# Attention's feature sums on two half-array column tiles: an attention and mixture kernel on one Trainium2 core

## The chip, the cores and the metric

The kernel runs on one core of one Trainium2 chip. Its time is the device time of that core in microseconds (us). A core has a TensorE for matrix products (in the profile PE for the matmuls and PEld for the weight loads that precede them), a VectorE (DVE), a ScalarE (ACT), a GpSimd (POOL) and a SyncE (SP), from whose queue this kernel starts its transfers.

## What is computed

Attention with exponential features over 8 batches of 8 heads, 576 tokens and 64 values a head, then a gated feed-forward layer on the 4608 tokens. All is float32.

```python
def phi(x):
    proj = np.einsum('bhsd,df->bhsf', x, w_phi)          # 64 -> 128
    proj = proj - np.max(np.abs(proj), axis=-1, keepdims=True)
    return np.concatenate([np.exp(proj), np.exp(-proj)], axis=-1)
q_p, k_p = phi(q), phi(k)
kv  = np.einsum('bhsf,bhsd->bhfd', k_p, v)               # the sums of features and values
z   = np.sum(k_p, axis=2)
num = np.einsum('bhsf,bhfd->bhsd', q_p, kv)
den = np.einsum('bhsf,bhf->bhs', q_p, z)[..., None] + 1e-06
x = num / den                                            # as 4608 tokens of 512
xn = x / rms(x) * rms_g
out = (silu(xn @ w_gate) * (xn @ w_val)) @ w_out         # 512 -> 1536 -> 512
```

The change concerns `kv` and `z`. They are computed as one: the values carry a 65th column of ones, which gives `z`.

## The kernel before

Heads are taken two at a time, so attention has 32 pairs. A loop over the pairs keeps four of them in flight: in iteration i it runs `front` of pair i (transposes and projections of keys and queries), `mid` of pair i-1 (exponentials and the sums), `back` of pair i-2 (numerators and denominators) and `last` of pair i-3 (the division and the store). Each is a list of small functions with places between about 0 and 1 of an iteration; `_merge` runs them in the order of these places. `mid` is spread evenly from -0.2 to 1.1. Beside them go the decoding of weights and, from iteration 9 on, `fill` products of the feed-forward layer (lines L489 before). The framework then orders each engine's instructions once more, by what is ready, so the calls of one function needn't stay together in an engine's queue; the listings below are of this final order. After attention, which ends at about 485 us, come the feed-forward layer's first products (L565) and its last (L1259).

The 576 tokens of a head are 4 blocks of 128 (`T0`) and a rest of 64; the rests of the two heads share one block. For each sign sg of the exponent, `mid` adds up in the tile `acc` (128 features x 2 signs x 2 heads x 65): `kvr(sg)`, one product for the rests of both heads (`er` with `vr`, 130 columns), and `kv(h, sg)`, four products for a head's blocks (`ek` with `vm`, 65 columns). With `kvr` that is 2 + 16 = 18 products for a pair. In each, the exponentials (128 tokens x 128 features, float32) are the weight that is loaded into TensorE, and the values are streamed through. Their order in `mid` before is

```python
rexp, kexp(0), qexp("q", 0), kvr(0), kv(0, 0), kexp(1), qexp("r", 0),
qexp("q", 1), kv(1, 0), (kvr(1), kv(0, 1)), kv(1, 1), kvs_
```

`kexp` and `rexp` make the exponentials of the keys on ACT, `qexp` transposes the queries' projections on TensorE and makes their exponentials on ACT and their low parts on POOL. `kvs_` copies `acc` into the tiles kv0 or kv1 (high part on ACT, low part on DVE), which `back` reads. There is one `acc`; the buffers of `ek` are two, one for each head, so that the next pair's `kexp` needs the sums of this one done.

Of the kernel before, what the change touches and what calls it, by code (L numbers as in the profile page):

```python
# [58 lines left out]
def _split(nc, hi, lo, x, hi_copy=None, lo_eng=None):  # L59
    (hi_copy or nc.scalar.copy)(hi, x)  # L60
    (lo_eng or nc.vector).tensor_tensor(lo, x, hi.bitcast(F32), ALU.subtract)  # L61
# [21 lines left out]
def kernel(ctx: ExitStack, tc: tile.TileContext, q, k, v, w_phi,  # L83
                         w_gate, w_val, w_out, rms_g, out):
    nc = tc.nc
# [7 lines left out]
    T0 = S // 128  # L93
# [104 lines left out]
    make_identity(nc, ident)  # L198


    const.tile([128, 32], F32, name="pad0")
    wh = const.tile([128, 2 * F], F32R, name="wh")
    wl = const.tile([128, 2 * F], F32R, name="wl")
# [123 lines left out]
    def mid(pr):  # L327
        d = st[pr]
        y, vm, vr, (kh, kl) = d["y"], d["vm"], d["vr"], d["kv"]
        acc = ps_k.tile([128, 2, 2, D + 1], F32, name="acc")  # L330
        qh = big.tile([128, 2, 2, S], F32R, name="qh")
        ql = big.tile([128, 2, 2, S], F32R, name="ql")
        d.update(qh=qh, ql=ql)
        er = wk.tile([128, 2, F], F32, name="er")
        e = {}

        def kexp(h):
            e[h] = wk.tile([128, 2, T0, F], F32, name="ek")
            for sg in range(2):
                nc.scalar.activation(e[h][:, sg], y["k", h], AF.Exp, scale=1.0 - 2.0 * sg)  # L340

        def rexp():
            for sg in range(2):
                nc.scalar.activation(er[:, sg], y["r", 0][:, 0], AF.Exp, scale=1.0 - 2.0 * sg)


        def kvr(sg):
            nc.tensor.matmul(acc[:, sg].rearrange("p h d -> p (h d)"), er[:, sg],
                             vr.rearrange("p s d -> p (s d)"), start=True, stop=False)

        def kv(h, sg):
            for j in range(T0):
                nc.tensor.matmul(acc[:, sg, h], e[h][:, sg, j], vm[:, h, j],  # L353
                                 start=False, stop=(h == 1 and j == T0 - 1))

        def kvs_():
            av = acc.rearrange("p a h d -> p h a d")
            _split(nc, kh[:, :, :, 0:D + 1], kl[:, :, :, 0:D + 1], av)
            if pr == PR - 1:
                for x in (kh, kl):  # L360
                    nc.vector.tensor_copy(x[:, :, :, D + 1:128], x.bitcast(F32)[:, :, :, D:D + 1].broadcast_to([128, 2, 2, 127 - D]))


        def qexp(n, h):
            m = 4 if n == "q" else 1
            yp = ps_s.tile([128, 512], F32, name="sm")
            for j in range(m):
                src = y[n, h][:, j] if n == "q" else y[n, h][:, 1]
                nc.tensor.transpose(out=yp[:, j * 128:(j + 1) * 128], in_=src, identity=ident)  # L369
            if n == "q":  # L370
                hi, lo = qh[:, :, h, 0:SM], ql[:, :, h, 0:SM]
                eq = wk.tile([128, 2, 512], F32, name="eq")
                ei, yi = eq, yp
            else:
                hi, lo = qh[:, :, :, SM:S], ql[:, :, :, SM:S]
                eq = wk.tile([128, 2, 128], F32, name="eqr", bufs=1)
                ei = eq.rearrange("p a (h s) -> p a h s", h=2)
                yi = yp[:, 0:128].rearrange("p (h s) -> p h s", h=2)
            for sg in range(2):
                nc.scalar.activation(ei[:, sg], yi, AF.Exp, scale=1.0 - 2.0 * sg)  # L380
                nc.scalar.activation(hi[:, sg], yi, AF.Exp, scale=1.0 - 2.0 * sg)  # L381
                if n == "q":
                    for c in range(0, SM, SM // 2):
                        cs = slice(c, c + SM // 2)
                        nc.gpsimd.tensor_tensor(lo[:, sg, cs], ei[:, sg, cs], hi[:, sg, cs].bitcast(F32), ALU.subtract)  # L385
            if n != "q":
                nc.gpsimd.tensor_tensor(lo, ei, hi.bitcast(F32), ALU.subtract)  # L387

        return [
            rexp,  # L390
            lambda: kexp(0),
            lambda: qexp("q", 0),
            lambda: kvr(0),
            lambda: kv(0, 0),
            lambda: kexp(1),
            lambda: qexp("r", 0),
            lambda: qexp("q", 1),
            lambda: kv(1, 0),
            lambda: (kvr(1), kv(0, 1)),
            lambda: kv(1, 1),  # L400
            kvs_,
        ]

# [114 lines left out]
    for i in range(PR + 3):  # L518
        streams = []
        if i < PR:  # L520
            streams.append(_spread(front(i), -0.2, 0.7))
        if 0 <= i - 1 < PR:
            streams.append(_spread(mid(i - 1), -0.2, 1.1))
        if 0 <= i - 2 < PR:
            streams.append(back(i - 2))
        if 0 <= i - 3 < PR:
            streams.append(last(i - 3))
        dq += 0.8 if i < 10 else 1.1
        dl, decs = decs[:int(dq)], decs[int(dq):]
        dq -= int(dq)  # L530
        streams.append(dl)
        if i < PR:
            _merge(streams)
        if len(units) <= 6:
            landed(nc.vector if i < PR else nc.gpsimd)
        if i >= FIRST:
            quota += (N // TF * J1 * 2 - RES - TAIL) / (PR - FIRST) if i < PR else TAIL / 3
            nf = min(int(quota + 1e-6), len(units))
            quota -= nf
            now, units[:] = units[:nf], units[nf:]  # L540
            _merge([now] if i < PR else streams + [_spread(now, 0.0, 0.75)])
        load_x()
        if i + 2 < PR:
            load(i + 2)
        if i in (20, 22):
            raw_gv((i - 20) // 2)
# [113 lines left out]
    nc = Engines()  # L660
# [513 lines left out]
    nc = tc.nc  # L1174
# [155 lines left out]
```

## Time and profile before

| | |
|---|---|
| median of 2 runs | 1246.05 us (1245.63 to 1246.46) |
| the profiled execution | 1252.8 us, span 1251.0 us, mean granted clock of TensorE 0.992 |
| PE, PEld busy | 1219.3 us (97%), 1208.1 us (97%), 10355 records each |
| DVE, ACT, POOL busy | 1037.2 (83%), 803.9 (64%), 832.2 us (67%) |
| sums, `kv` (L353) | 1024 matmuls, busy 131.2 us, mean 269 ns of one |
| sums, `kvr` (L348) | 128 matmuls, busy 26.3 us, mean 287 ns of one |

In such a profile a line as `L353 PE MATMUL acc<-vm,ek 128x65` names the line of the kernel, the engine, the operation, the tile written and those read, and the shape streamed. Busy times of matmuls overlap: a matmul's record lasts from its start to the modelled end of its results, and the next starts long before. What one costs is therefore read from the distance between starts, not from its length. In rows of time order the first number is the start, the second the length of the whole merged group, and xN the count.

### The profile page before, as it was taken

The page shows a single profiled execution, that of the slowest core. Times are in us where ns is not written, and L with a number is a line of the kernel's source. Part 1 is how long each engine was busy: PE and PEld are TensorE (multiplying, and loading weights), DVE is VectorE, ACT ScalarE, POOL GpSimd, SP SyncE. Part 2 cuts the span into 40 slices and gives each one's busy share as a digit, 9 for nine tenths or more (in the row PEclk, how much of TensorE's full clock was granted, in tenths as well). Part 3 has the DMA queues.
Part 4 walks back from the last instruction along what each step waited for, and adds up shares of the span by engine and source line. Part 5 has one row for each costly group of instructions (what it writes and reads, how often), then busy time and mean ns, then how long its engine had stood idle before and what let it go on. Part 6 is the DMA issues. An engine that isn't in the chain of part 4 may idle for free. (4 is left out here: it accounts for less than half of the span.)

```text
span 1251.0 us, 28462 instructions
## 1 busy us (share of the span) xinstructions
PE 1219.3 (97%) x10355; PEld 1208.1 (97%) x10355; DVE 1037.2 (83%) x1498; ACT 803.9 (64%) x1867; POOL 832.2 (67%) x774
## 2 busy tenths in 40 slices
PE   8999999999999998999999999999999899999998
PEld 7988999989999998999999999999999899999998
DVE  6888977678788886687997887988775889999995
ACT  6887887768788786667666667756655443433432
POOL 3654654456556666674876766787655578888885
PEclk9998999999999998999999999999999899999999
DMA  5545565766665654686466656566544544444531
GB/s 151 130 132 147 136 202 147 192 171 165 178 172 141 181 150 152 219 255 198 133 196 189 205 187 214 177 196 191 180 138 130 182 149 155 153 135 141 167 116 51
DMA packets 199752, 206.55 MB, mean 165 GB/s; under 512 B 70334, under 2 KB 169790, under 8 KB 197436
## 3 DMA queue, kind: packets, MB, share of 16 engines
q1 hardware_dynamic: 199612, 204.73, 54.5%
q8 instruction: 82, 1.34, 0.4%
q14 instruction: 58, 0.48, 0.1%
HBM read 135.18 MB, written 69.49 MB: 164 GB/s over the span
## 5 line engine op out<-in xcount | busy, mean ns | idle before, releaser
L385 POOL TENSOR_TENSOR ql<-eq,qh 128x256 fp32r<-128x256 f32 x256 | 215.6, 873 | 94.7 <-issue 59.0
L565 PE MATMUL B<-xo,w 128*128 128x256 f32 x1458 | 195.5, 278 | 2.5 <-DVE c L565 1.8
L565 PEld LDWEIGHTS B<-xo,w 128*128 128x128 f32 x1458 | 180.0, 188 | 4.0 <-DVE c L565 2.6
L61 POOL TENSOR_TENSOR xo<-st,xo 128x768 fp32r<-128x768 f32 x52 | 122.3, 2366 | 35.4 <-ACT xo L60 31.7
L314 DVE TENSOR_REDUCE mx<-pp 128x4 f32<-128x512 f32 (+1 forms) x160 | 101.0, 633 | 52.7 <-PE pp L312 51.2
L60 ACT CAST xo<-st 128x768 fp32r<-128x768 f32 x54 | 43.5, 836 | 150.1 <-DVE st L1209 73.7
L565 PE MATMUL E<-xo,w 128*128 128x256 f32 x972 | 137.7, 277 | 0.0
L565 PE MATMUL A<-xo,w 128*128 128x256 f32 x972 | 137.7, 277 | 0.0
L353 PE MATMUL acc<-vm,ek 128*128 128x65 f32 x1024 | 131.2, 269 | 0.0
L353 PEld LDWEIGHTS acc<-vm,ek 128*128 128x128 f32 x1024 | 127.3, 193 | 0.0
L565 POOL TENSOR_TENSOR h<-h,c 128x256 f32<-128x256 f32 x81 | 65.7, 811 | 91.3 <-ACT h L565 68.9
L565 PEld LDWEIGHTS A<-xo,w 128*128 128x128 f32 x972 | 123.5, 188 | 0.3
L565 PEld LDWEIGHTS E<-xo,w 128*128 128x128 f32 x972 | 123.4, 188 | 0.1
L381 ACT ACTIVATE qh<-sm 128x512 fp32r<-128x512 f32 (+1 forms) x192 | 96.9, 505 | 0.0
L61 POOL TENSOR_TENSOR xo<-w,xo 128x768 fp32r<-128x768 f32 x36 | 90.9, 2524 | 7.4 <-ACT xo L60 7.4
L310 PE MATMUL pp<-wh,th 128*128 128x256 f32 x288 | 87.7, 306 | 3.4 <-DVE yk L317 1.2
L380 ACT ACTIVATE eq<-sm 128x512 f32<-128x512 f32 x128 | 78.2, 611 | 18.4 <-PE sm L369 17.8
L312 PE MATMUL pp<-wh,tl 128*128 128x256 f32 x288 | 84.2, 301 | 0.0
L311 PE MATMUL pp<-wl,th 128*128 128x256 f32 x288 | 82.0, 286 | 0.0
L565 ACT ACTIVATE h<-A 128x256 f32<-128x256 f32 x81 | 31.1, 385 | 77.6 <-PE A L565 64.1
L1259 PE MATMUL gy<-w,xo 128*128 128x256 f32 x648 | 78.8, 280 | 1.3 <-ACT xo L60 1.3
L387 POOL TENSOR_TENSOR ql<-eqr,qh 128x256 fp32r<-128x256 f32 x32 | 25.5, 798 | 81.9 <-ACT qh L381 74.0
(190 smaller groups left out, 3602.9 us busy)
## 6 DMA issues: line engine op xcount, KB each, us to landing
w<-hs SPq DMA_DIRECT2D x17, 1536.0 KB
hs<-h SPq DMA_DIRECT2D x81, 256.0 KB
gvs<-fo SPq DMA_DIRECT2D x108, 128.0 KB
gvr<-gvs SPq DMA_DIRECT2D x54, 256.0 KB
x<-xs SPq DMA_DIRECT2D x18, 512.0 KB
x<-xs SPq DMA_DIRECT2D x9, 1024.0 KB
rc<-di SPq DMA_DIRECT2D x31, 288.0 KB
kt<-in_k_dram SPq DMA_DIRECT2D x32, 256.0 KB
```

The source lines that it names most:

```text
L60: (hi_copy or nc.scalar.copy)(hi, x)
L61: (lo_eng or nc.vector).tensor_tensor(lo, x, hi.bitcast(F32), ALU.subtract)
L310: nc.tensor.matmul(o, th[:, cs], wh, start=True, stop=False)
L311: nc.tensor.matmul(o, th[:, cs], wl, start=False, stop=False)
L312: nc.tensor.matmul(o, tl[:, cs], wh, start=False, stop=True)
L314: nc.vector.tensor_reduce(mx[:, 0:2 * m], pp[:, 0:2 * m], axis=AX.X, op=ALU.max, apply_absolute_value=True)
L353: nc.tensor.matmul(acc[:, sg, h], e[h][:, sg, j], vm[:, h, j], start=False, stop=(h == 1 and j == T0 - 1))
L380: nc.scalar.activation(ei[:, sg], yi, AF.Exp, scale=1.0 - 2.0 * sg)
L381: nc.scalar.activation(hi[:, sg], yi, AF.Exp, scale=1.0 - 2.0 * sg)
L385: nc.gpsimd.tensor_tensor(lo[:, sg, cs], ei[:, sg, cs], hi[:, sg, cs].bitcast(F32), ALU.subtract)
L565: r = f(*a, **k)
L1259: nc.tensor.matmul(place[n], a[:, kp], w[:, o], start=(first and (kp, i) == turns[0]), stop=((kp, i) == turns[-1]), skip_group_check=True)
```

## The change

Each of the 18 products is cut in two along the features: columns 0 to 63 of the weight go to partitions 0 to 63 of `acc`, columns 64 to 127 to partitions 64 to 127. In the program the two halves are matmuls on array tiles of 128 rows x 64 columns, at columns 0 and 64; all others are on the whole array of 128 x 128. The same values are streamed for both. The products of a pair are no longer spread over `mid` but issued by one function, `kvall`, behind all exponentials of the pair and ahead of `kvs_`; `mid` has 8 entries instead of 12, over the same places.

```diff
+    halves = slice(0, 64), slice(64, 128)
...
         def kvr(sg):
-            nc.tensor.matmul(acc[:, sg].rearrange("p h d -> p (h d)"), er[:, sg],
-                             vr.rearrange("p s d -> p (s d)"), start=True, stop=False)
+            for f in halves:
+                nc.tensor.matmul(acc[f, sg].rearrange("p h d -> p (h d)"), er[:, sg, f],
+                                 vr.rearrange("p s d -> p (s d)"), start=True, stop=False)
 
         def kv(h, sg):
             for j in range(T0):
-                nc.tensor.matmul(acc[:, sg, h], e[h][:, sg, j], vm[:, h, j],
-                                 start=False, stop=(h == 1 and j == T0 - 1))
+                for f in halves:
+                    nc.tensor.matmul(acc[f, sg, h], e[h][:, sg, j, f], vm[:, h, j],
+                                     start=False, stop=(h == 1 and j == T0 - 1))
+
+        def kvall():
+            for sg in range(2):
+                kvr(sg)
+                kv(0, sg)
+                kv(1, sg)
...
             lambda: qexp("q", 0),
-            lambda: kvr(0),
-            lambda: kv(0, 0),
             lambda: kexp(1),
             lambda: qexp("r", 0),
             lambda: qexp("q", 1),
-            lambda: kv(1, 0),
-            lambda: (kvr(1), kv(0, 1)),
-            lambda: kv(1, 1),
+            kvall,
             kvs_,
```

TensorE's queue before, pair 28 of 32, where its sums begin (`pp` are projections, `sm` transposes, `fp` fill products; `vr_149`, `vm_146` the pair's values):

```order
L310 MATMUL pp<-wh,th 128x256
L311 MATMUL pp<-wl,th 128x256
L348 MATMUL acc<-vr_149,er 128x130
L489 MATMUL fp<-xo,fv 128x256
L369 MATMUL sm<-ident,yr 128x128
L312 MATMUL pp<-wh,tl 128x256
L310 MATMUL pp<-wh,th 128x256
L311 MATMUL pp<-wl,th 128x256
L312 MATMUL pp<-wh,tl 128x256
L353 MATMUL acc<-vm_146,ek 128x65 x4
```

The first sum of the pair, on the rests, stands alone there; four of the first head's blocks follow seven rows later. The same pair's beginning with the change (`acc` is now written 64 features at a time, on lines L350 and L356; L425 is `back`'s numerators of pair 26, which read kv0; L494 the fill products):

```order
L350 MATMUL acc<-vr_149,er 64x130 x2
L425 MATMUL sm<-qh,kv0h 128x320
L425 MATMUL sm<-ql,kv0h 128x320
L425 MATMUL sm<-qh,kv0l 128x320
L425 MATMUL sm<-qh,kv0h 128x320
L425 MATMUL sm<-ql,kv0h 128x320
L425 MATMUL sm<-qh,kv0l 128x320
L494 MATMUL fp<-xo,fg 128x256 x10
```

The two halves of the rests' product stand alone again, and numerators of pair 26 have come in behind them.

The end of the sums of pair 28 before, up to the first numerator of pair 27, which reads kv1:

```order
L297 MATMUL sm<-ident,rb 128x128
L489 MATMUL fp<-xo,fv 128x256 x7
L353 MATMUL acc<-vm_146,ek 128x65 x4
L348 MATMUL acc<-vr_149,er 128x130
L353 MATMUL acc<-vm_146,ek 128x65
L297 MATMUL sm<-ident,kt 128x128 x4
L353 MATMUL acc<-vm_146,ek 128x65 x7
L420 MATMUL sm<-qh,kv1h 128x320
```

And with the change:

```order
L378 MATMUL sm<-ident,yq 128x128 x4
L356 MATMUL acc<-vm_146,ek 64x65 x6
L298 MATMUL sm<-ident,rb 128x128
L356 MATMUL acc<-vm_146,ek 64x65 x7
L350 MATMUL acc<-vr_149,er 64x130 x2
L356 MATMUL acc<-vm_146,ek 64x65 x2
L298 MATMUL sm<-ident,kt 128x128 x4
L356 MATMUL acc<-vm_146,ek 64x65 x14
L494 MATMUL fp<-xo,fv 128x256 x3
L425 MATMUL sm<-qh,kv1h 128x320
```

The sums of the second sign and most of the first have moved together towards the end, with a transpose (`rb`, `kt`) still between them: here runs of 6, 11 and 14 half products where there were runs of 6 and 7 whole ones. Over the whole queue the 576 whole products before stand in 145 unbroken runs, the 1152 halves in 181.

## Prediction

> **What bounds the kernel now.** The first view is the page's head and its slices; the digits of PE (TensorE's matmuls) and PEld (its weight loads) are read against DVE's.
>
> ```profile
> span 1251.0 us, 28462 instructions
> PE 1219.3 (97%) x10355; PEld 1208.1 (97%) x10355; DVE 1037.2 (83%) x1498; ACT 803.9 (64%) x1867; POOL 832.2 (67%) x774
> PE   8999999999999998999999999999999899999998
> DVE  6888977678788886687997887988775889999995
> ```
>
> TensorE is the busy one in nearly every slice. A busy PE is not yet PE at its peak, so the next views ask what paces it. The sums of this change lie in the first part of the run, which the view of the sums' tile shows; the windows of that part show how full each engine is there.
>
> ```profile
> L353 PEld LDWEIGHTS acc<-vm,ek x1024: 186/192/333, 15.8 to 484.7; 128*128 128x128 f32 x171
> L353 PE MATMUL acc<-vm,ek x1024: 217/275/417, 15.9 to 484.8; 128*128 128x65 f32 x171
> L348 PE MATMUL acc<-vr,er x128: 272/275/329, 15.7 to 482.0; 128*128 128x130 f32 x128
> ...
> core 0: us, PE busy (x) PEld busy (x) DVE busy (x) ACT busy (x) POOL busy (x), PEclk, DMA share, GB/s
> ...
> 300.00:350.00 50.00, 49.94 (x427) 49.72 (x427) 41.64 (x76) 41.10 (x103) 30.91 (x38) 1.00 0.59 159
> ...
> sum 350.00, PE 345.70 PEld 342.87 DVE 283.26 ACT 277.85 POOL 199.38; mean PE 49.39 PEld 48.98 DVE 40.47 ACT 39.69 POOL 28.48
> ```
>
> The sum is over the seven windows from 100 to 450 us. TensorE is busy in 345.7 of 350 us there, the next engine (DVE) in 283.3, which is 81%. So attention goes at TensorE's pace: time added to TensorE's stream there lengthens the kernel one for one, and time taken out shortens it one for one until about 19% of those 485 us, some 90 us, are gone. The view of waits agrees: all those of TensorE in 100 to 460 us come to 4.3 us (the first number of each row).
>
> ```profile
> PE sm L369 <- DVE tl L61: 2.1, 2, 1.8
> PE pp L310 <- DVE yq L317: 1.1, 1, 1.1
> PE sm L369 <- ACT xo L60: 0.5, 1, 0.5
> PE pp L310 <- DVE yr L317: 0.3, 1, 0.3
> PE sm L297 <- DVE tl L61: 0.3, 1, 0.3
> ```
>
> Next, what paces a single sum. The rows of time order show weight loads and matmuls of one pair's sums, and a stretch of wide matmuls from the chain of waits in the last stage.
>
> ```profile
> 300.19 1.87 PEld L353 LDWEIGHTS acc<-vm,ek 128*128 128x128 f32 x16
> 300.30 1.90 PE L353 MATMUL acc<-vm,ek 128*128 128x65 f32 x16
> 1152.68 4.08 PE gz L1259 x36
> ```
>
> The 16 loads begin (1.87 - 0.192) / 15 = 0.112 us apart, the last load's own 0.192 us taken off. The wide matmuls, 256 columns each, follow one another at 4.08 / 36 = 0.113 us. So a product with 65 columns costs TensorE as much as one with 256. Streaming the columns is not what costs: the shortest matmul of 130 columns takes 272 ns and that of 65 takes 217 ns, so 65 columns are 55 ns and half of the 112 ns go by without streaming. **The load of a 128-column weight, at 0.112 us, sets the pace of the sums.** Each product in the code makes two loads and two matmuls (1024 + 128 records for 32 pairs of 18 products, where 32 x 18 = 576). The sums hold TensorE for 1152 x 0.112 = 129 us, a tenth of the kernel.
>
> **The change, part by part.**
>
> *Halves.* Each product becomes two, with weights of 64 columns and the same 65 or 130 columns streamed: 2304 loads and 2304 matmuls where there were 1152. No row shows a load of 64 columns, nor two loads at once, so the price is bounded. Below: a half load takes half of 0.112 us and the two halves load and stream at once, so that a pair of halves costs 0.056 us (its streaming, 55 ns, just fits); that saves 1152 x 0.056 = 64.5 us. In the middle: half loads one after another, 2 x 0.056 = 0.112, which saves nothing. Above: a half load takes as long as a whole one and they follow one another, 2304 x 0.112 = 258 us, an added 129 us. I take the lower end, since the 0.112 us is where the row of loads shows the time to go, and each half writes other partitions of the tile `acc` through another half of the array.
>
> The Trainium skill, page TensorE: Matmul & The Clock Gate, section LDWEIGHTS, says that a load's time goes by its columns, P / 1.2 ns; that is 107 ns for 128 columns, where the trace has 112. By that figure a half load would be 53 ns, an estimate, and the saving 1152 x 0.059 = 68 us in place of 64.5. The Trainium skill, page TensorEngine Tiling (Array Packing), section Key Properties, adds that different tiles can load and multiply in parallel; no run here shows it yet.
>
> *The grouping.* The code issues a pair's products in one call, but the program's order is another matter: over the whole listing of TensorE the 1152 half products lie in 181 runs, about 5.7 to a pair, with transposes, projections and fill products between; 32 runs were what one call per pair might suggest. Before, the 576 whole products lay in 145 runs, but a run's edge changed nothing in the array's shape. Of the 181 runs, 104 have an odd count, so that a half stands without a partner and costs 0.056 us more: 5.8 us. The saving falls to 58.7 us.
>
> *The switches.* Each run now has an edge into the two-column-tile shape and an edge out of it, 362 in all. The trace of before has no such edge, so it is bounded too. Below: nothing. Above: at an edge the matmul before must end before the next load begins. Going in, behind a matmul of 256 columns (rows below, 277 to 280 ns), the next one starts after 277 + 56 = 333 ns in place of 113, so 220 ns are lost. Going out, behind one of 65 columns, 217 + 112 = 329 in place of 112, so 217 ns are lost. A run then costs 0.437 us, and 181 of them 79 us.
>
> ```profile
> L565 PE MATMUL A<-xo,w 128*128 128x256 f32 x972 | 137.7, 277 | 0.0
> L1259 PE MATMUL gy<-w,xo 128*128 128x256 f32 x648 | 78.8, 280 | 1.3 <-ACT xo L60 1.3
> ```
>
> Between them: only the loading ahead is lost, so that the load begins when the last matmul has streamed. Going in that is about 56 ns, going out 55 ns (one load less its cover, one stream), so 0.11 us per run and 20 us in all. I take the upper end: it is the one whose terms are lengths that the rows show, of matmuls that run to their end, and nothing in the trace shows an instruction of one shape starting while another shape is in flight.
>
> The Trainium skill speaks against this change at this place: the page TensorEngine Tiling (Array Packing), section Key Properties, says that changing the tiling mode, and not merely the tile, drains the engine. With it the sum below stands at +20; without it the sum would be -59, and no row of the trace decides between the two.
>
> *Moved work.* Mid's list shrinks from 12 entries to 8, so the exponentials and transposes of the queries move a little within an iteration, and all sums come behind `kexp(1)`. Only TensorE instructions are in the moved calls: no DMA, and no wait on SP's or POOL's queues is added by them. The exponentials of the keys (128 activations, below) have more time before they are needed; the next pair's `kexp(0)` needs the buffers that the sums read, and comes at 1.04 iterations where the sums start at 0.86. An iteration is 485 / 32 = 15 us, so 0.18 of it, 2.8 us, is its room, less than the 4 us of a pair's sums. ACT may wait there a microsecond or so a pair; with ACT at 278 of 350 us this is covered, and if it were not, 32 x 1 us would show as TensorE waiting at `L311` for the projections.
>
> ```profile
> L340 ACT ACTIVATE ek<-yk x128: 611/648/701, 10.3 to 478.5; 128x512 f32<-128x512 f32 x128
> ```
>
> *Sum.* -64.5 (halves) + 5.8 (odd halves) + 79 (switches) = **+20 us** against the profiled execution's 1252.8 us (span 1251.0). That one lies 6.8 us above the median of the runs, 1246.05; the difference is carried over to the median: 1266 us.
>
> **The rivals.**
>
> *Slower: the halves load in turn.* If TensorE takes the weights of one half after the other's, 2304 x 0.056 = 129 us, nothing is saved and the switches stay: 1246 + 79 = 1325 us. For it: in every stretch above the loads follow one another at 0.112 us and never lie closer, whatever streams beside them, which looks like one path for weights. Against: all those loads go to the same columns. It decides wherever the starts of half loads within a run lie 0.056 us apart on average and not 0.028.
>
> *Faster: the edges are cheap.* If the halves do run at once and an edge costs between nothing and 0.11 us a run, the sum is -59 to -39: 1187 to 1207 us. For it: the trace's matmuls overlap by more than half of their length, so the array is made to hold several in flight. DVE's 81% would allow it.
>
> *Half the overlap.* A half's two loads follow one another in program order, then the other half's two. If only neighbours can overlap, one load in two finds a partner, and 29 us are saved in place of 59: 1296 us with the full edges, 1237 with cheap ones.
>
> *Turn by turn with cheap edges.* No saving and 0 to 20 us of edges: 1246 to 1266, no change.
>
> *The half load isn't half.* 129 us more, and edges: 1375 to 1454 us.
>
> That the change doesn't do what it says is partly a fact: one run it is not. In 32 runs the edges would cost 14 us and the forecast would be about 1196.
>
> **How the numbers follow.** Forecast (at once, full edges) 0.28, its own range 1250 to 1280. In turn with full edges 0.22. At once with cheap edges 0.18. Half the overlap 0.14, of which 0.09 with full edges. In turn with cheap edges 0.12. Whole-length half loads 0.06. A change of 2%, 25 us, is about what a measurement of this kernel can tell from none. Faster: 0.18. Within 2%: 0.28 + 0.05 + 0.12 = 0.45. Slower: 0.22 + 0.09 + 0.06 = 0.37. The range goes from 1196 to 1330 us: it holds all but the last case and the lower half of the fast one, 0.15 together.
>
> **What would show it.** In the profile after, the sums' lines (L350, L356) have 256 + 2048 records each of loads and matmuls. Halves at once: inside a run of ten or more, half matmuls start 0.028 us apart on average; in turn 0.056; if not halved 0.112. Edges: from a 256-column matmul to the first half 0.33 us and from the last half to the next whole load 0.33 us in place of 0.11. TensorE remains without waits in 100 to 450 us, and everything after attention keeps its length. I am wrong if attention's end, at 485 us now, moves by over 30 us either way, or if the stages behind it change by over 5 us.

## The result and the profile after

The changed kernel takes 1266.42 us in the median of 2 runs (1263.46 to 1269.38), 1.0146 of the time before, with a 95% interval of 1.0109 to 1.0183. Run once more in a larger comparison, the ratio was 1.0114 (1.0073 to 1.0155). The two medians differ by 20.4 us, the profiled spans by 16.6, and the other comparison gives 14: slower by 14 to 20 us, which is less than 2%. The forecast was 1266.

The page's head, and from the windows the row of 100 to 450 us (the columns are those of the windows of before):

```profile
span 1267.6 us, 30758 instructions
PE 1233.1 (97%) x11507; PEld 1179.5 (93%) x11507; DVE 1035.4 (82%) x1498; ACT 808.7 (64%) x1867; POOL 832.7 (66%) x774
...
100.00:450.00 350.00, 343.85 (x3690) 312.49 (x3690) 278.72 (x494) 272.43 (x679) 194.11 (x242) 1.00 0.58 164
```

TensorE is as busy as before (343.85 us where it was 345.70), but the weight loads, PEld, fell from 342.87 to 312.49: the array now spends time in which it loads nothing. All of TensorE's waits in 100 to 460 us add up to 6.3 us, where it was 4.3, so the pace is still TensorE's own. The sums' lines show the doubled counts and the shorter loads (median 137 ns, where it was 192):

```profile
L356 PEld LDWEIGHTS acc<-vm,ek x2048: 132/137/231, 16.1 to 498.5; 128*64 128x64 f32 x187
L356 PE MATMUL acc<-vm,ek x2048: 219/222/315, 16.3 to 498.5; 128*64 128x65 f32 x187
...
L350 PE MATMUL acc<-vr,er x256: 274/276/478, 15.9 to 495.4; 128*64 128x130 f32 x128
```

The last sum starts at 498.5 us, 13.7 later than before; the feed-forward layer's products `A<-xo,w` start at 599.0 us, 17.0 later, and the span is 16.6 longer. Nearly all of the loss comes in attention.

Time order in one pair, matmuls first and then loads, from a transpose through three runs of halves (14, 12 and 28 matmuls) to the next numerators:

```profile
298.78 0.60 PE L378 MATMUL sm<-ident,yq 128*128 128x128 f32 x4
299.31 0.68 PE L356 MATMUL acc<-vm,ek 128*64 128x65 f32 x14
299.92 0.33 PE L298 MATMUL sm<-ident,rb 128*128 128x128 f32 x1
300.18 0.34 PE L356 MATMUL acc<-vm,ek 128*64 128x65 f32 x4
300.34 0.39 PE L350 MATMUL acc<-vr,er 128*64 128x130 f32 x4
300.57 0.29 PE L356 MATMUL acc<-vm,ek 128*64 128x65 f32 x4
300.78 0.66 PE L298 MATMUL sm<-ident,kt 128*128 128x128 f32 x4
301.37 1.04 PE L356 MATMUL acc<-vm,ek 128*64 128x65 f32 x28
302.34 0.42 PE L425 MATMUL sm<-qh,kv0h 128*128 128x320 f32 x1
302.59 0.31 PE L425 MATMUL sm<-ql,kv0h 128*128 128x320 f32 x1
...
301.37 0.90 PEld L356 LDWEIGHTS acc<-vm,ek 128*64 128x64 f32 x28 [0.17 <-issue]
302.33 0.19 PEld L425 LDWEIGHTS sm<-qh,kv0h 128*128 128x128 f32 x1
```

*Halves side by side.* The 28 loads start (0.90 - 0.137) / 27 = 0.028 us apart. In single records two partners start 7 ns apart and the next two 0.058 us later. A pass over both halves thus costs 0.058 us where a whole product's pass cost 0.112. The four matmuls of 130 columns take 0.39 us, so their second pair starts (0.39 - 0.276) = 0.11 us after the first: there the streaming sets the pace, and halving the load saves nothing.

*The edges.* The last record of the run of 28 ends at 301.37 + 1.04 = 302.41; with the 0.219 us of the shortest such matmul it started at 302.19. The next whole load starts at 302.33, 0.14 us later, where before a load started together with the matmul ahead of it. The last transpose of four ends at 300.78 + 0.66 = 301.44, so it started at 301.17 (0.273 us each), and the first half load follows 0.20 us later. A matmul of 65 columns streams for 0.055 us and a transpose is followed by the next after 0.11: at both edges the next load begins 0.09 us after the streaming has ended. Behind a 256-column matmul, where 96 of the 181 edges going in lie, the first half load begins 0.204 us after that matmul's start, in the median; such matmuls follow one another at 0.113, so it is 0.09 us there too. (They read tiles of the type float32r. The 0.85 ns a column of the float32 sums, 55 ns for 65, doesn't hold for them: 256 columns would take 0.217 us.) The 0.09 us is longer than if only loading ahead were lost, and shorter than waiting for the modelled end.

Over the whole program, starts taken from the trace (where a record is longer because the matmul waited in it for its load, the excess is added to its start), the 181 edges going in are 0.257 us in the median and 46.8 us in sum, those going out 0.258 us and 47.8 us, starts of matmul to matmul. The account of TensorE's time:

| | before | after |
|---|---|---|
| from one sum to the next, within a run | 113.7 us | 70.4 us |
| from a run's last sum to what follows | 16.0 us (145 edges) | 47.8 us (181) |
| into a run, above the 0.113 us of two whole matmuls | 0 | 46.8 - 181 x 0.113 = 26.3 us |
| sum | 129.7 us | 144.5 us |

The sums cost TensorE 14.8 us more, of the 16.6 that the span grew. Where the other 1.8 us come from isn't shown.

### The profile page after: what moved, and what is told of

It reads as the page before. It is cut to its first block, busy times and chain, and to the rows that moved or that the text cites. A ratio compares the mean times of both kernels' runs of the same rounds, so it can differ in the third digit from the quotient of the medians.

```text
span 1267.6 us, 30758 instructions
## 1 busy us (share of the span) xinstructions
PE 1233.1 (97%) x11507; PEld 1179.5 (93%) x11507; DVE 1035.4 (82%) x1498; ACT 808.7 (64%) x1867; POOL 832.7 (66%) x774
## 4 chain that ended last, share of the span: by engine, by line
PE 86%; DVE 6%; DMA 5%; ACT 1%; issue 1%; SPq 1%; POOL 0%; DVEq 0%; ACTq 0%
PE B L570 13%; PE E L570 11%; PE A L570 11%; PE gd L1264 6%; PE gz L1264 6%; PE gy L1264 5%; PE fp L494 5%; PE acc L356 5%; PE sm L425 4%; PE fp L425 3%; PE pp L313 3%; PE fp L1264 3%; PE pp L311 3%; PE sm L298 2%; PE pp L312 2%; PE sm L378 2%
## 5 line engine op out<-in xcount | busy, mean ns | idle before, releaser
L356 PE MATMUL acc<-vm,ek 128*64 128x65 f32 x2048 | 105.6, 228 | 0.4 <-ACT ek L341 0.4
L356 PEld LDWEIGHTS acc<-vm,ek 128*64 128x64 f32 x2048 | 84.7, 138 | 21.0 <-issue 9.0
L313 PE MATMUL pp<-wh,tl 128*128 128x256 f32 x288 | 86.8, 304 | 5.9 <-DVE tl L61 5.9
L341 ACT ACTIVATE ek<-yk 128x512 f32<-128x512 f32 x128 | 75.0, 649 | 4.3 <-PE acc L356 2.2
```

Source lines behind the costliest of these rows:

```text
L313: nc.tensor.matmul(o, tl[:, cs], wh, start=False, stop=True)
L356: nc.tensor.matmul(acc[f, sg, h], e[h][:, sg, j, f], vm[:, h, j], start=False, stop=(h == 1 and j == T0 - 1))
```

## The experiments

Two theories were set against each other. The theory: halves do load and stream at once, and what they save is spent at some 0.35 us a run at the edges. The rivals: the edges are cheap and the moved work costs the time; or the halves take turns; or the order, not the halves, decides. Three questions follow: what the change's two parts do alone, whether neighbours in one half also overlap, and whether fewer runs win.

**The grouping alone.** One call for a pair's sums, as in the change, but whole products:

```diff
-    halves = slice(0, 64), slice(64, 128)
+    halves = slice(0, 128),
```

> The grouping alone: one call for a pair's sums behind all exponentials, as in the change, but 18 whole products. No halves, no edges. Theory: within 6 us of before. Rival D: carries the change's 15 us or a good part of it.

Measured 1.0051 of before (1.0010 to 1.0092), 6 us with an interval of 1 to 12. So the grouping of whole products is not quite free, and costs less than the change. It isn't shown that these 6 us are part of the change's loss: TensorE's waits in 10 to 500 us come to 18.6 us here and 15.3 before, but to 11.6 with the change, and the next run loses as much without the grouping.

**The halves alone**, in the order of before:

```diff
             lambda: qexp("q", 0),
+            lambda: kvr(0),
+            lambda: kv(0, 0),
             lambda: kexp(1),
...
-            kvall,
+            lambda: kv(1, 0),
+            lambda: (kvr(1), kv(0, 1)),
+            lambda: kv(1, 1),
```

> All products in halves but in the order of before, spread over mid: the grouping undone. Its queue holds 192 runs where the change has 181. Theory: the grouping in the code hardly moves the time: 11 x 0.35 = 4 us above the change, 1.014 to 1.025 of before. Rival D (the grouping is what hurts or helps, by the waits of the exponentials): more than 12 us from the change, either way.

Measured 1.0142 (1.0059 to 1.0225), against 1.0114 of the change in the other comparison; the two can't be told apart, and rival D's 12 us of difference are not there. Its 192 edges going in sum to 49.7 us and those going out to 49.2, the same 0.26 us each. Undoing the grouping changed the number of runs by 11 of 181, since the final order cuts them anyway.

**Edges without a saving.** The kernel before, with only the products on the rests in halves:

```diff
-            nc.tensor.matmul(acc[:, sg].rearrange("p h d -> p (h d)"), er[:, sg],
-                             vr.rearrange("p s d -> p (s d)"), start=True, stop=False)
+            for f in (slice(0, 64), slice(64, 128)):
+                nc.tensor.matmul(acc[f, sg].rearrange("p h d -> p (h d)"), er[:, sg, f],
+                                 vr.rearrange("p s d -> p (s d)"), start=True, stop=False)
```

> The kernel before, in its own order, with only the 64 products on the rests (130 columns) in halves; the 512 others stay whole. Each of the 64 is an island of two halves, with two edges, and its own two passes cost 0.110 us each as before, so nothing is saved. Theory (0.35 us for each island's two edges): 64 x 0.35 = 22 us more than before, 1.8%. Rival A (edges are cheap, the change's loss came from moved work): within 5 us of before. The prediction's full edge price (0.44): 28 us more.

Measured 1.0138 (1.0068 to 1.0209), 17 us with an interval of 9 to 26. That holds the 22 us of the theory; rival A's 5 us lie below it and the prediction's 28 us just above. An island of four half matmuls and its two edges:

```profile
304.57 0.44 PE L349 MATMUL acc<-vr,er 128*64 128x130 f32 x4
304.94 1.11 PE L354 MATMUL acc<-vm,ek 128*128 128x65 f32 x8
...
304.57 0.20 PEld L349 LDWEIGHTS acc<-vr,er 128*64 128x64 f32 x4
304.94 0.97 PEld L354 LDWEIGHTS acc<-vm,ek 128*128 128x128 f32 x8 [0.17 <-issue]
```

The final order made 72 islands of the 64 products. Their edges sum to 17.2 us in and 21.7 us out; less 0.113 and the 0.110 of their own streaming, that is 38.9 - 72 x 0.223 = 22.9 us, 0.32 us an island. A kernel with none of the saving and two fifths of the edges loses as much as the change. That settles it against the rival of cheap edges.

**One run for a pair.** TensorE's instructions of attention listed before a pair's sums are held ahead of them, those listed after behind them:

```diff
+    @contextmanager
+    def one_run():
+        with ExitStack() as es:
+            for i in ordered.since:
+                es.enter_context(tc.issue_after(i))
+            yield
+        ordered.since.clear()
+        ordered.last = newest()
...
         def kvall():
-            for sg in range(2):
-                kvr(sg)
-                kv(0, sg)
-                kv(1, sg)
+            with one_run():
+                for sg in range(2):
+                    kvr(sg)
+                    kv(0, sg)
+                    kv(1, sg)
```

(`ordered` stands for TensorE in attention; it keeps each of its instructions behind `last` and notes it in `since`. In the rows of these kernels L341 is the line of this helper, so the tiles tell the work.)

> The change with TensorE's queue held so that the 36 half products of a pair stand in one unbroken run, 32 runs in place of 181. Theory (halves load and stream at once, 0.058 us a pass; each run costs 0.34 us at its two edges): the changed kernel's 1266 us less 149 x 0.34 = 51 and less 6 for the halves without a partner, about 1209, plus whatever the stricter order costs in waits (0 to 15). Rival A (the edges are cheap, and the added time comes from the moved exponentials and waits): no better than 1255. Rival B (the halves take turns, nothing is saved inside a run): not below 1255 either, since 32 edges add 11 us to 1246.

Measured 1.0121 (1.0038 to 1.0204), the change's own time: the expectation of 1209 failed. By the time alone rivals A and B, who said not below 1255, would be right. It isn't for the halves, though, as the rows of one pair show, where 32 matmuls start within 0.9 us; and rival A has failed in the islands above. The last row is that of the windows:

```profile
312.95 0.44 PE L382 MATMUL acc<-vr,er 128*64 128x130 f32 x4
313.22 1.10 PE L388 MATMUL acc<-vm,ek 128*64 128x65 f32 x32
314.15 0.39 PE L382 MATMUL acc<-vr,er 128*64 128x130 f32 x4
314.38 1.10 PE L388 MATMUL acc<-vm,ek 128*64 128x65 f32 x32
315.41 1.65 PE L341 MATMUL fp<-xo,fv 128*128 128x256 f32 x12
...
100.00:450.00 350.00, 311.10 (x3503) 293.08 (x3501) 268.46 (x488) 267.85 (x663) 189.78 (x241) 0.96 0.58 159
```

A pair's sums fill 315.41 - 312.95 = 2.46 us, where 36 passes of 0.112 were 4.03. Counted as in the table above, the sums cost 72.3 us within the runs, 7.9 going out and 8.2 - 32 x 0.113 = 4.6 going in, 84.8 us instead of 129.7. But TensorE is now busy in only 311 of 350 us. Its longest waits, here in 10 to 500 us, are for the copies of `acc`, for the low parts of the transposes and for `yk`, the projections of the keys with their maximum taken off:

```profile
PE sm L341 <- DVE kv1l L61: 16.0, 8, 6.9
PE pp L341 <- DVE tl L61: 8.4, 15, 1.8
PE fp L341 <- DVE kv0l L61: 7.1, 4, 3.2
PE pp L341 <- DVE yk L318: 6.6, 12, 0.9
```

The waits aren't all. The granted clock (PEclk, the number behind POOL's in a window's row) is 0.96 in 100 to 450 us, against 0.99 before and 1.00 with the change. Rows from a stretch with half the clock and from just behind it, and the window of that stretch:

```profile
206.31 0.41 PE L341 MATMUL pp<-wh,th 128*128 128x256 f32 x1
206.53 0.41 PE L341 MATMUL pp<-wl,th 128*128 128x256 f32 x1
...
210.71 0.28 PE L341 MATMUL pp<-wh,th 128*128 128x256 f32 x1
210.83 0.28 PE L341 MATMUL pp<-wl,th 128*128 128x256 f32 x1
...
204.00:210.00 6.00, 5.34 (x24) 5.35 (x25) 3.33 (x7) 2.77 (x7) 0.89 (x2) 0.50 0.81 237
```

With the clock at 0.50 two matmuls of 256 columns start 0.22 us apart, behind it 0.12. Over the whole span the mean granted clock is 0.983 of 1280.3 us, so 22 us would be lost by it if TensorE always had work, and 0.992 of 1251.0 us before, 10 us. By this estimate up to 12 us of the missing gain went to the clock. In these runs the clock is lower where TensorE waits more (1.00 with 344 us busy of 350, 0.96 with 311); that the waits bring it down was not tested.

**The strict order alone**, the same with `halves = slice(0, 128),`:

> The same strict order, one run for a pair, but 18 whole products on the whole array as before. It prices the order alone. Theory: 1246 to 1261 (no saving, no edges, some waits by the stricter order). Rival C (the gain of one_run comes from the order, not from the halves): as fast as one_run within 10 us.

Measured 1.0109 (1.0035 to 1.0183). The order by itself costs some 14 us, at the upper end of the expected 0 to 15 (1246 to 1261 against 1246); TensorE is busy in 330 of the 350 us. Its sums cost 128.4 us, so the halves take 128.4 - 84.8 = 43.6 us from TensorE beside it, and the two kernels still can't be told apart in time (1.0121 and 1.0109). Rival C's number, within 10 us, thus came true, but there was no gain to come from the order. Under this order TensorE's work alone no longer sets the time.

**Neighbours in one half.** As one run, with all 18 products of the first half ahead of all 18 of the second:

```diff
...
-                for sg in range(2):
-                    kvr(sg)
-                    kv(0, sg)
-                    kv(1, sg)
+                for f in halves:
+                    for sg in range(2):
+                        kvr(sg, (f,))
+                        kv(0, sg, (f,))
+                        kv(1, sg, (f,))
```

> As one_run, but all 18 products of the first half come before all 18 of the second, so that no half has its partner beside it; instructions and edges are the same in number. Theory: two neighbours in the same half can't load at once, so each of 2048 passes takes 0.058 us alone and 256 passes of 130 columns 0.110: 147 us for the sums in place of 74, 73 us more than one_run, about 1280. Rival B (turns in any case): the same time as one_run.

```profile
302.07 0.44 PE L382 MATMUL acc<-vr,er 128*64 128x130 f32 x2
302.35 1.09 PE L388 MATMUL acc<-vm,ek 128*64 128x65 f32 x16
```

The 16 matmuls start (1.09 - 0.222) / 15 = 0.058 us apart, twice the 0.028 of partners side by side. The sums' distances grow from 72.3 to 140.4 us, 68 more (73 expected). The time went up by far less, to 1.022 (1.0147 to 1.0293), 12 us above one run: TensorE's added work filled its waits (busy 340 of 350 us). Of the missing 56 us, 43 are time for which TensorE was idle in one run and is busy here (458.3 and 501.2 us in the first 520). The clock can be the rest: its mean is 0.983 in one run and 0.996 here, up to 17 us by the same estimate. The overlap thus needs two different halves.

**The change once more**, in the same comparison.

> The changed kernel itself beside the others on one chip, for comparison: 1263 to 1269 us, ratio to before 1.011 to 1.018. Every theory expects this.

Measured 1.0114 (1.0073 to 1.0155), as expected.

**Five attempts to keep long runs and lose the waits.** With `mid` in another order, sums and copy at about half an iteration, mid's end drawn in to 0.95:

```diff
-            rexp,
-            lambda: kexp(0),
+            lambda: (rexp(), kexp(0)),
+            lambda: kexp(1),
             lambda: qexp("q", 0),
-            lambda: kexp(1),
+            lambda: (kvall(), kvs_()),
             lambda: qexp("r", 0),
             lambda: qexp("q", 1),
-            kvall,
-            kvs_,
```

> As one_run (36 halves in one unbroken run for a pair), with the sums and their copy placed earlier, about half an iteration ahead of the numerators that need them, so that TensorE needn't wait for the copy. Theory: the saving of one run a pair (sums and edges some 88 us in place of 130) shows in the time once the waits of one_run (some 50 us on the copies kv0l, kv1l and on projections) are gone: 1215 to 1235 against 1246 to 1255. Rival E (with the sums in one block the other engines have too little to do at once, wherever it stands): no faster than before.

Measured 1.0238 (1.0160 to 1.0316), no faster than before, as rival E said. TensorE no longer waits for the copies. But ACT now waits 30.8 us in 100 to 450 for the sums to free the buffers of `ek`, and its copies come behind these exponentials in its queue; DVE stands behind the copies, and the low parts of the transposes come late. The first row is for 10 to 500 us, the others for 100 to 450:

```profile
PE pp L341 <- DVE tl L61: 34.5, 27, 2.4
...
DVE kv0l L61 <- ACT kv0h L60: 16.8, 10, 3.3
DVE kv1l L61 <- ACT kv1h L60: 13.5, 10, 1.6
```

With the later work left free to move ahead of the sums (`ordered.last` is not set):

> As one_run, 32 unbroken runs of 36 halves, but TensorE's order is held on one side alone: a run comes behind the work that the code lists before it, while the work listed after it may still be moved ahead of it. Theory (halves and edges save some 40 us of TensorE's time in attention, and one_run lost that in waits by its strict order): part of the saving shows, 1225 to 1255, below one_run by 15 us or more, with less than 30 us of waits on TensorE. Rival E (a block of sums of this length leaves the other engines waiting whatever the order): the same as one_run within 8 us.

Measured 1.0283 (1.0212 to 1.0353). TensorE is busy in 307.7 of 350 us, and its longest wait is again for kv1l (22.7 us in 10 to 500). The theory missed, and rival E too: it is some 20 us slower than one run.

With the 12 TensorE instructions listed last before the sums left free (`ordered.since[:-12]`):

> Held on both sides like one_run, but the 12 TensorE instructions listed last before the sums are left free, so that the sums fall into 54 runs in place of 32. Theory: edges cost 54 x 0.35 = 19 us in place of 11, 8 more than one_run, and the waits get less by more than that: 1235 to 1265. Rival E: the same as one_run plus 8 us.

Measured 1.0112 (1.0025 to 1.0198), 1265 us where before is 1251, with TensorE busy in 313.7 of 350 us. The slack came out level with the change and with one run, at the upper end of what was expected. The waits in 100 to 450 us fell by only 3 us against one run (35.5 and 38.6), not by more than the 8 us of added edges; the interval excludes neither the theory nor rival E.

With the places written out, the sums at 0.4 and the copy at 0.75, held strictly, and with the slack:

> As one_run (32 unbroken runs, held on both sides), with the parts of mid at places chosen against the two waits seen so far: the sums at 0.4 of an iteration, their copy at 0.75, so that neither the numerators wait for the copy (one_run) nor DVE and ACT for the sums ahead of the copy (one_run_early). Theory: TensorE's waits in 100 to 450 us fall from some 40 us to below 20, and the time to 1225 to 1250, faster than before by up to 2%. Rival E: the waits move to other work and the time stays at 1265 to 1290.

> The same places with the slack of 12 instructions ahead of the sums; 60 runs, so 28 more pairs of edges, 10 us, against one_run_lag. Theory: waits below 15 us, 1225 to 1250. Rival E: 1260 to 1285.

Measured 1.0455 (1.0381 to 1.0529) and 1.0504 (1.0438 to 1.0571), the slowest of all. TensorE waits for the low parts of the transposes once more (30.8 and 32.0 us in 100 to 450). Rival E's times were too short, but its statement held: the waits moved. Beside the waits the granted clock was lower: 0.91 in 100 to 450 us of the first of the two, against 0.99 before. Its mean over the span is 0.958 of 1317.7 us, 55 us by the estimate used for one run, where before has 10. So up to 45 of the 57 us that this kernel lost may be the clock's.

```profile
PE pp L341 <- DVE tl L61: 30.8, 22, 2.7
PE pp L341 <- DVE yq L318: 7.8, 7, 2.1
...
100.00:450.00 350.00, 302.28 (x3171) 285.05 (x3170) 248.19 (x447) 246.45 (x608) 176.85 (x222) 0.91 0.52 146
```

None of the versions beats the kernel before. Whether a better order of attention could turn the 44 us into time stays open; these runs show only that six orders with long runs don't.

## Why the prediction was right, point by point

- **What bounds the kernel.** Held for the change: TensorE's waits stayed at some 6 us and the sums' added time appears in the span. The sentence that time taken out shortens the kernel one for one, up to some 90 us, didn't hold in any run that took time out, though each of them changed the order too. DVE's 81% leaves room on average only. In one run the low copies on DVE begin 2.3 us after the high ones have ended, in the mean (1.0 before), and DVE is idle for only 0.14 us ahead of them: they stand behind other work in its queue. The granted clock, which fell beside the waits, is not in the prediction.
- **The halves at once.** Right: 0.028 us between starts, as forecast for that case. The term was too large all the same: 58.7 us expected, while in the account above the passes cost 129.7 - (70.4 + 181 x 0.058) = 48.8 less. What was wrong is the price of the 128 passes with 130 columns, put at 0.056 us: they stream for 0.110 and saved nothing, 7 us. The other passes take 0.058 us, which is 2 us more.
- **Unbroken runs.** The 181 runs and the halves without partner stand as counted.
- **The edges.** That an edge costs time, and that no load of one shape begins while a matmul of the other still streams, is right; the size isn't: 79 us were expected, and 26.3 + (47.8 - 181 x 0.058) = 63.6 measured, 0.35 us a run. The upper bound took the modelled end of the last matmul (0.217 us after its start) as the time from which a load may begin; it begins 0.14 us after the start of a 65-column matmul. The working of the out edge was also off by itself, since it set 329 ns against a whole pass and not against the half pass that had been put in the sum. The Trainium skill's sentence that changing the mode drains the engine (TensorEngine Tiling (Array Packing), Key Properties) agrees with the 0.09 us at the edges; so does its sentence that tiles load and multiply in parallel, with the 7 ns between partners.
- **Moved work.** Put at nothing. The grouping of whole products measured 6 us; with the halves no price of it is seen (11.6 us of waits, fewer than before, and the same loss without it).
- **The sum.** +20 was forecast; 48.8 saved and 63.6 spent are +14.8, and 14 to 20 were measured. That 1266 was hit to the microsecond is luck: the saving was put 10 us too large and the edges 15, errors that work against each other, and the profiled spans differ by 16.6, not by 20.
- **The rivals.** Halves in turn, cheap edges and the half overlap are excluded by the rows. The remark that 32 runs would give about 1196 is refuted in the only way tried: with 32 runs the sums' time on TensorE fell as computed, and the time of the kernel didn't.

## What to carry to other kernels

Where weight loads pace short matmuls, two half-array tiles do halve the pass (0.112 to 0.058 us here), but each stretch of them costs two edges: count the unbroken stretches in the final order of the queue, not in the code. Here a stretch has to hold more than 0.35 / 0.054, some 7 passes of both halves, to pay; the 1152 passes of the change lie in 181 stretches, 6.4 in the mean, and 128 of them save nothing. And a busy engine that is held to a fixed order to keep its stretches whole can lose all that it saves, in waits and in a lower granted clock, with its neighbours busy for less than 80% of the time: read both before naming the cause.

## What the runs showed of the hardware

Two matmuls on the two column halves start 7 ns apart, with their loads as close. A 65-column float32 pass of two halves takes 0.058 us, that of a whole product 0.112. At a change between the whole array and the halves, in either direction, the next load begins some 0.09 us after the last streaming ends. A matmul that waits for its load has a record that is longer by the wait (0.275 in place of 0.217 us), so its start alone misleads by 58 ns. With the granted clock at 0.50, matmuls of 256 columns start 0.22 us apart in place of 0.12.
